# The last gate of a turning cycle behind the next cycle's first sum, with operand, weight and attention work moved to other cycles and steps

## The chip, the cores and the metric

The kernel runs on one core of a Trainium2 chip. The metric is the device time of one execution in microseconds (us); less is better. Engines are named as in the profile: PE multiplies matrices, DVE is the vector engine, ACT the scalar engine, POOL the third elementwise engine, SP the engine that issues all DMAs here.

## What is computed

Chunk attention on 8 x 576 tokens, then two feed-forward layers on the 4608 tokens that come out of it. The reference, cut:

```python
def _attn_ref(q, k, v):                    # q, k, v: 8 x 8 heads x 576 x 64
    chunk = 64
    scores = scale * np.matmul(q_c, k_c.transpose(0, 1, 2, 4, 3))
    attn = np.exp(scores - scores.max(-1, keepdims=True))
    attn = attn / (np.sum(attn, axis=-1, keepdims=True) + 1e-09)
    return np.matmul(attn, v_c).reshape(B, H, S, D)

def _moe_ref(x, w_in, w_out, alpha):       # 4608 x 512, 512 x 2048, 2048 x 512
    h = x @ w_in
    g = np.maximum(h, 0.0) + alpha * np.minimum(h, 0.0)
    return g @ w_out

def _moe2_ref(x, w_in, w_out):
    h = x @ w_in
    return (h - np.tanh(h)) @ w_out
```

The four weight matrices arrive as float64, and the kernel turns each into float32 with integer operations on its words before it uses it.

## The kernel before

Every product is made of three passes: operand and weight are each split into a high part (rounded to the type that PE multiplies fast) and a low part, and high x high, low x high and high x low are summed. The 4608 tokens are 9 blocks of 512; the 2048 features of a layer are 16 groups of 128.

**Layer one, blocks 0 to 6**, is 112 steps. A step multiplies one feature group up (`up`, 12 matmuls, L547) and multiplies the group of two steps earlier down into four accumulators y0 to y3 (`down`, 12 matmuls, L617), through `next_down`. At steps 49, 65, 81 and 97 (and others of that form) the down work is the last of a block, and `finish` copies the four accumulators to stage tiles `yst` (ACT, L642) and stores them to `ysc` (SP, L643). The stage pool has three tiles, which `neg` and `xst` use too, so the fourth copy waits until the first store has landed. All else is woven in by a table: `at(step, fn, ..., place=)` appends to `events[step]`, and `step_one` fires the places 1 and 2, then `up`, place 0, `down`, place 3, the gate `act_g`, the block's stores, and place 4. The table carries

- the attention of the later token tiles: loads into `raw` (`some_loads`, L340, 32 DMAs of SP for a unit of tiles), transposes (`att_a` on DVE, L385; `att_a_natural` on PE, L358, for the tiles 8, 13, 31 and 22, copied by DVE L359 and ACT L360), scores `sc` (L400), weights `p`, and the product with v into `xp` (L471). `tr`, `sc` and `xp` share one PSUM tile pair, tag "a", so each waits for the readers of the last.
- the *parks*: the second layer's weights converted, combined into the seven operands of a fast 2 x 2 block product, split, and written to device memory for later. `park_load` (SP, L206, tile `rw`), `park_form` (DVE conversions, POOL sums L222, L230), `park_split` (ACT L254, POOL L255, tiles `whi`, `mr`), `park_store` (SP, L266). Sixteen of the kinds "u1"/"u" follow each other every four steps from step 36; the first six of kind "d" (weights of the down product) come after them.

**The pair stage** (`two_blocks`) takes two blocks at a time. Pair s=0 is layer one's blocks 7 and 8, s=1 to 4 are layer two's pairs, each of 8 cycles p=0 to 7; eight half-wide cycles (`small`) for the last block follow. A cycle makes four 128 x 512 results from seven products (p1, p5, p6, p2, p3, p7, p4, of 6 matmuls each, L1196) instead of eight. Its sums: `copy` H0 and p5 (ACT, L1206), `add(H1, X, p5)` after p6 and `add(Y, X, p5)` after p7 (DVE, L1203). H1 is what p3 goes on to accumulate in, and X, which add(Y) reads, is what p4 overwrites. Each result goes through a `Gate`: `square`, `second`, `edge` on ACT, `drain` on DVE (L595, L596, which frees the PSUM bank), `close` on DVE (L606 to L608, two inputs in SBUF). The gates are c11, c12, c22 and c21 in this order. Between the products stand 48 down matmuls (24 for s=0), in the numbers that `gaps` gives; a plain cycle of layer two has 12 of them before p4 and 36 after. For s > 0 the cycles p=0 and p=4 are *turning* cycles (`turns`): the accumulators change from one block of the pair to the other, and 12 down matmuls stand ahead of p1's sum and 12 behind it.

`on(s, p, place, fn)` hangs further work on a cycle (`run` fires it): for the next pair `turn`, `put(product, operand)` (two ACT copies L698 and two subtractions L700 for the two halves) and `tokens(o, a, b)` (two subtractions, L710); loads of them (`load_y`); and the last ten "d" parks, one to a cycle. `c21.close()` is the last thing a cycle gives DVE ahead of its `end` hooks, and the next cycle's add(H1) stands behind both.

## Time and profile before

| | us |
|---|---|
| median of three runs | 1693.98 (1693.06 to 1698.06) |
| the profiled execution | 1695.32 |
| its span in the trace | 1693.5 |
| PE busy | 1619.7 (96%) |
| DVE busy | 1232.0 (73%) |
| ACT busy | 986.9 (58%) |
| POOL busy | 458.8 (27%) |

The profiled execution stands 1.34 us above the median. A PE of 96% leaves 74 us in which it was idle; the busy time itself holds matmuls that ran at a lower clock for a while after a gap. The chain of waits, the sum of PE's waits by cause and the start of each cycle's first product tell where these are.

### The profile page before, as it was taken

The page shows a single profiled execution, that of the slowest core. Times are in us where ns is not written, and L with a number is a line of the kernel's source. Part 1 is how long each engine was busy: PE and PEld are TensorE (multiplying, and loading weights), DVE is VectorE, ACT ScalarE, POOL GpSimd, SP SyncE. Part 2 cuts the span into 40 slices and gives each one's busy share as a digit, 9 for nine tenths or more (in the row PEclk, how much of TensorE's full clock was granted, in tenths as well). Part 3 has the DMA queues.
Part 4 walks back from the last instruction along what each step waited for, and adds up shares of the span by engine and source line. Part 5 has one row for each costly group of instructions (what it writes and reads, how often), then busy time and mean ns, then how long its engine had stood idle before and what let it go on. Part 6 is the DMA issues. An engine that isn't in the chain of part 4 may idle for free.

```text
span 1693.5 us, 26409 instructions
## 1 busy us (share of the span) xinstructions
PE 1619.7 (96%) x9309; PEld 1329.5 (79%) x9309; DVE 1232.0 (73%) x1860; ACT 986.9 (58%) x1769; POOL 458.8 (27%) x422
## 2 busy tenths in 40 slices
PE   7899999999999999999899899999999999999999
PEld 6688888878877887888677787787878777878887
DVE  7878857768777787743667788768886877688763
ACT  5756545455554555665566667575766676566553
POOL 1000002444334444322322223122222232222333
PEclk9999999999999999999999999999999999999999
DMA  9451426565565657477678735463555454544650
GB/s 261 153 189 39 107 69 139 131 171 140 141 149 141 153 147 233 146 258 229 217 235 297 250 108 174 139 199 103 181 162 178 127 159 150 164 136 156 216 160 25
DMA packets 339299, 276.49 MB, mean 163 GB/s; under 512 B 180432, under 2 KB 244960, under 8 KB 339168
## 3 DMA queue, kind: packets, MB, share of 16 engines
q1 hardware_dynamic: 339168, 274.82, 54.5%
q8 instruction: 73, 1.20, 0.3%
q14 instruction: 58, 0.48, 0.1%
HBM read 192.95 MB, written 81.79 MB: 162 GB/s over the span
## 4 chain that ended last, share of the span: by engine, by line
PE 69%; DVE 13%; ACT 5%; issue 5%; DMA 4%; SPq 3%; POOL 2%; DVEq 0%; ACTq 0%; POOLq 0%
PE y L1103 23%; PE hps L547 12%; PE y L617 12%; PE hpb L1196 10%; PE hps L1196 10%; SPq L340 2%; DVE arena L607 1%; DVE arena L606 1%; DMA ysc<-yst 1%; DVE g L560 1%; DVE arena L608 1%; DMA rw<-in_moe_w_in_dram 1%; DMA wu<-wu 1%; POOL glo L578 1%; DVE arena L595 1%
## 5 line engine op out<-in xcount | busy, mean ns | idle before, releaser
L578 POOL TENSOR_TENSOR glo<-arena,ghi 128x512 fp32r<-128x512 f32 x145 | 201.3, 1402 | 531.3 <-ACT ghi L575 354.3
L547 PE MATMUL hps<-x,w 128*128 128x512 f32 (+1 forms) x1356 | 328.4, 392 | 5.9 <-ACT kt L374 5.3
L547 PEld LDWEIGHTS hps<-x,w 128*128 128x128 f32 x1356 | 255.4, 190 | 59.6 <-ACT kt L374 5.8
L1103 PE MATMUL y<-w,ghi 128*128 128x512 f32 x1152 | 296.7, 390 | 0.0
L1196 PE MATMUL hpb<-w,wu 128*128 128x512 f32 (+1 forms) x912 | 218.3, 383 | 35.7 <-DVE hpb L1203 32.7
L1103 PEld LDWEIGHTS y<-w,ghi 128*128 128x128 f32 x1152 | 215.4, 188 | 43.7
L617 PE MATMUL y<-ghi,w 128*128 128x512 f32 x880 | 233.0, 398 | 6.3 <-ACT yst L642 6.3
L1196 PEld LDWEIGHTS hpb<-w,wu 128*128 128x128 f32 x912 | 165.9, 192 | 73.6 <-DVE hpb L1203 37.2
L1196 PE MATMUL hps<-w,wu 128*128 128x512 f32 (+1 forms) x912 | 215.7, 382 | 3.6 <-ACT hpb L1206 2.1
L1196 PEld LDWEIGHTS hps<-w,wu 128*128 128x128 f32 x912 | 168.0, 194 | 39.9 <-ACT hpb L1206 4.8
L617 PEld LDWEIGHTS y<-ghi,w 128*128 128x128 f32 x880 | 162.8, 189 | 42.3 <-ACT yst L642 7.6
L1103 PE MATMUL y<-w,glo 128*128 128x512 f32 x576 | 163.2, 390 | 1.0 <-POOL glo L578 1.0
L560 DVE SCALAR_TENSOR_TENSOR g<-neg,nalpha_sb,g 128x512 f32<-128x512 f32 x112 | 94.2, 841 | 54.9 <-ACT g L559 54.8
L617 PE MATMUL y<-glo,w 128*128 128x512 f32 x440 | 126.7, 391 | 0.1
L1103 PEld LDWEIGHTS y<-w,glo 128*128 128x128 f32 x576 | 107.8, 188 | 24.0 <-POOL glo L578 1.8
L578 DVE TENSOR_TENSOR glo<-g,ghi 128x512 fp32r<-128x512 f32 x111 | 95.9, 864 | 34.9 <-ACT ghi L575 33.8
L222 POOL TENSOR_TENSOR whi<-w 128x256 f32<-128x256 f32 x32 | 26.3, 845 | 333.3 <-DMA ysc<-yhalf 234.0
L575 ACT ACTIVATE ghi<-g 128x512 fp32r<-128x512 f32 x112 | 70.5, 630 | 78.2 <-DVE g L560 77.9
L558 ACT ACTIVATE neg<-hps 128x512 f32<-128x512 f32 x112 | 66.3, 592 | 76.9 <-PE hps L547 76.7
L608 DVE COPY_PREDICATED arena<-ktc,th 128x512 f32<-128x512 uint32 x118 | 97.9, 830 | 10.2 <-ACT ktc L602 0.6
L599 ACT ACTIVATE w<-sq,bias_sb 128x512 f32<-128x512 f32 x144 | 104.0, 722 | 0.0
L602 ACT ACTIVATE ktc<-sq,edge_sb 128x512 f32<-128x512 f32 x144 | 103.8, 721 | 0.0
(173 smaller groups left out, 2497.0 us busy)
## 6 DMA issues: line engine op xcount, KB each, us to landing
wu<-wu SPq DMA_DIRECT2D x336, 256.0 KB, 3.2
g<-arena SPq DMA_DIRECT2D x67, 256.0 KB, 3.6
arena<-g SPq DMA_DIRECT2D x65, 256.0 KB, 3.8
raww<-in_moe_w_in_dram SPq DMA_DIRECT2D x16, 512.0 KB, 5.4
v<-in_v_dram SPq DMA_DIRECT2D x32, 256.0 KB, 3.8
raww<-in_moe_w_out_dram SPq DMA_DIRECT2D x16, 512.0 KB, 5.3
rw<-in_moe_w_in_dram SPq DMA_DIRECT2D x16, 512.0 KB, 5.0
wu<-whi SPq DMA_DIRECT2D x32, 256.0 KB, 2.6
```

The lines of the kernel that those rows point to most:

```text
L340: nc.sync.dma_start(out=o, in_=i)
L547: nc.tensor.matmul(out=hp[:, cols], lhsT=w[:, a, m], rhs=x[b][:, kk, cols], start=(kk == 0 and i == 0), stop=(kk == KD - 1 and i == 2),)
L558: nc.scalar.activation(out=neg, in_=hp, func=AF.Relu, scale=-1.0)
L560: nc.vector.scalar_tensor_tensor(out=g, in0=neg, scalar=nalpha_sb[:, f:f + 1], in1=g, op0=ALU.mult, op1=ALU.add)
L575: nc.scalar.activation(out=hi, in_=g, func=AF.Copy)
L578: lo_engine.tensor_tensor(out=lo, in0=g, in1=hi.bitcast(F32), op=ALU.subtract)
L599: nc.scalar.activation(out=self.w, in_=self.sq, func=AF.Square, bias=bias_sb)
L602: nc.scalar.activation(out=self.mask, in_=self.sq, func=AF.Relu, bias=edge_sb)
L608: nc.vector.copy_predicated(g, self.mask.bitcast(U32), self.th)
L617: nc.tensor.matmul(out=acc[t], lhsT=lhsT, rhs=rhs, start=(f == ends[0] and i == 0), stop=(f == ends[1] and i == 2))
L1103: nc.tensor.matmul(out=self.acc[t], lhsT=lhsT, rhs=rhs, start=(self.f == self.ends[0] and i == 0), stop=(self.f == self.ends[1] and i == 2),)
L1196: nc.tensor.matmul(out=o, lhsT=w[:, a, c], rhs=x[c][:, b, :h], start=start and i == 0 and c == 0, stop=i == 2 and c == 1, skip_group_check ...
```

## The change

1. **att_a_natural** of tiles 13, 31 and 22 is fired two steps before the tile's scores instead of one (13: step 29 instead of 30; 31: 56 instead of 57; 22: 65 instead of 66), and the loads of the unit behind it may begin a step sooner. `some_loads` leaves out the steps 49, 65, 81 and 97.
2. **Parks of kind u**: the load moves from place 4 of a step to place 2 of the next, form and split of "u1" from place 2 to place 4 of the step before, and the store of "u" from place 4 to place 1 of its step. At a block's end that puts it, and the load, ahead of the block's `ysc` stores on SP.
3. **Border of s=0**: `turn`, put p1 and two `tokens` move from the last cycle to the end of the one before; the other operands are spread over p6, p7, p4 and the end of the last cycle, all on DVE, with two extra tile pairs e1 and e2.
4. **Borders of s >= 1**: `turn` and put p1 move from the end of p=4 to the end of p=5, a `tokens` from the end of p=5 to that of p=6, and the puts of p7 and p4 from the places p1 and p2 of the next pair's first cycle to its place p6.
5. **The ten last "d" parks** run three to two cycles, all within s=0 (before: one to a cycle, the last three in s=1, p=1 to 3).
6. **A turning cycle's** `c21.close()` and its `enlist` are put on `ends` and done in the next cycle, right behind add(H1).

```diff
@@ -755,14 +755,18 @@
     for unit in units:
         t = unit[0]
         if t % 9 == 4:
-            at(base[t] - 1, att_a_natural, t)
+            early = 1 if t < 3 * NPT else 2
+            at(base[t] - early, att_a_natural, t)
             at(free, load_natural_late, t)
-            free, apart = base[t], 1
+            free, apart = base[t] - early + 1, 1
         else:
             turn, apart = base[t] - (1 if t == 11 else apart), 2
             at(free, begin_unit, t, len(unit))
-            for r in range(free, turn):
-                at(r, some_loads, -(-32 // max(1, turn - 1 - free)))
+            loading = [r for r in range(free, turn) if r < 2 * KF or r % KF != 1]
+            loading = loading[:max(1, turn - 1 - free)]
+            for r in loading:
+                at(r, some_loads, -(-32 // len(loading)))
+            at(turn - 1, some_loads, 64)
             for i, tt in enumerate(unit):
                 at(turn + i, att_a, tt)
             free = turn + len(unit)
@@ -798,13 +802,13 @@
     at(2 * KF + 4, park_desk)
     for i in range(KF):
         n, c, step = i // 2, i % 2, 2 * KF + 4 + 4 * i
-        at(step, park_load, "u", n, c, place=4)
-        at(step + 2, park_form, "u1", n, c, place=2)
-        at(step + 2, park_split, "u1", n, c, place=2)
+        at(step + 1, park_load, "u", n, c)
+        at(step + 1, park_form, "u1", n, c)
+        at(step + 1, park_split, "u1", n, c)
         at(step + 3, park_store, "u1", n, c, place=4)
         at(step + 3, park_form, "u", n, c)
         at(step + 4, park_split, "u", n, c)
-        at(step + 5, park_store, "u", n, c, place=2 if i == KF - 1 else 4)
+        at(step + 5, park_store, "u", n, c, place=1)
     DP = 6
     for f in range(DP):
         step = 6 * KF + 5 + 2 * f
@@ -1241,44 +1245,45 @@
                 for name in names:
                     xs[m, name] = xs[m - 1, name]
 
+        V, G = nc.vector, nc.gpsimd
+
         def parks_done():
             spare.append(tuple(wide.tile([P, 2, 512], F32R, tag="w", name="xo") for _ in range(2)))
             new_slots(wide.tile([P, 2, 512], F32, tag="r", name="slots", bufs=1))
-
-        V, G = nc.vector, nc.gpsimd
+            raw["e1"] = [att.tile([P, NB], F32, tag=tag, name="e1") for tag in ("p", "pt")]
+            raw["e2"] = [vpool.tile([P, NB], F32, tag="v", name="e2") for _ in range(2)]
 
         def border(s):
             m = s + 1
             if s == 0:
                 on(s, 5, "p1", load_y, m, "b11", "b12")
                 on(s, 6, "p1", load_y, m, "b22", "b21")
-                on(s, 7, "start", turn, m)
-                for place, fn, args in (
-                    ("p1", put, ("p1", "b11", V)), ("p1", tokens, ("b11", "b12", "b11", V)),
-                    ("p5", put, ("p5", "b11", V)), ("p5", tokens, ("b11", "b22", "b11", V)),
-                    ("p6", put, ("p6", "b11", V)),
-                    ("p2", put, ("p2", "b21", V)), ("p2", tokens, ("b21", "b21", "b11", V)),
-                    ("p3", tokens, ("b12", "b22", "b12", V)), ("p3", put, ("p3", "b22", G)),
-                    ("p7", put, ("p7", "b12", G)),
+                on(s, 6, "end", parks_done)
+                on(s, 6, "end", turn, m)
+                for p, place, fn, args in (
+                    (6, "end", put, ("p1", "b11", V)), (6, "end", tokens, ("b11", "b12", "b11", V)),
+                    (6, "end", tokens, ("b12", "b22", "b12", V)),
+                    (7, "p6", put, ("p5", "b11", V)), (7, "p6", tokens, ("e1", "b22", "b11", V)),
+                    (7, "p7", put, ("p6", "e1", V)), (7, "p7", tokens, ("e2", "b21", "e1", V)),
+                    (7, "p4", put, ("p2", "b21", V)), (7, "end", put, ("p3", "b22", V)),
+                    (7, "end", put, ("p7", "b12", V)), (7, "end", put, ("p4", "e2", V)),
                 ):
-                    on(s, 7, place, fn, m, *args)
-                on(s, 7, "p3", drop, "b11")
-                on(s, 7, "p7", drop, "b22")
-                on(s, 7, "p7", drop, "b12")
-                on(s, 7, "end", put, m, "p4", "b21", V)
-                on(s, 7, "end", drop, "b21")
+                    on(s, p, place, fn, m, *args)
+                on(s, 7, "p7", drop, "b11")
+                on(s, 7, "end", drop, "b21", "b22", "b12")
+                on(s, 7, "end", lambda: [raw.pop(name) for name in ("e1", "e2")])
                 return
             on(s, 4, "p1", load_y, m, "b11", "b12")
             on(s, 5, "start", load_y, m, "b22", "b21")
-            on(s, 4, "end", turn, m)
-            on(s, 4, "end", put, m, "p1", "b11", V)
+            on(s, 5, "end", turn, m)
+            on(s, 5, "end", put, m, "p1", "b11", V)
             on(s, 5, "end", tokens, m, "b11", "b12", "b11", V)
-            on(s, 5, "end", tokens, m, "b12", "b22", "b12", V)
+            on(s, 6, "end", tokens, m, "b12", "b22", "b12", V)
             on(s, 6, "end", tokens, m, "e1", "b22", "b11", V)
             on(s, 6, "end", tokens, m, "e2", "b21", "e1", V)
             for p, place, product_, name in (
                 (7, "p1", "p5", "b11"), (7, "end", "p6", "e1"), (7, "end", "p2", "b21"), (7, "end", "p3", "b22"),
-                (8, "p1", "p7", "b12"), (8, "p2", "p4", "e2"),
+                (8, "p6", "p7", "b12"), (8, "p6", "p4", "e2"),
             ):
                 on(s + p // 8, p % 8, place, put, m, product_, name, V)
                 on(s + p // 8, p % 8, place, drop, name)
@@ -1289,14 +1294,17 @@
             border(s)
         on(0, 0, "start", park_load, "d", DP, 0)
         on(0, 0, "p5", park_store, "d", DP - 1, 0)
+        slips = (
+            (0, "p2", "p7", 0, "p4", 0, "p3"), (0, "end", "p6", 1, "p2", 1, "start"), (1, "p7", "end", 0, "start", 1, "p4"),
+        )
         for i, f in enumerate(range(DP, KF)):
-            s, p = (0, i) if i < 7 else (1, i - 6)
-            on(s, p, "p2", park_form, "d", f, 0)
+            p, form, split, later, store, latest, load = slips[i % 3]
+            p += 2 * (i // 3)
+            on(0, p, form, park_form, "d", f, 0)
+            on(0, p + later, split, park_split, "d", f, 0)
+            on(0, p + latest, store, park_store, "d", f, 0)
             if f + 1 < KF:
-                on(s, p, "p3", park_load, "d", f + 1, 0)
-            on(s, p, "p4", park_split, "d", f, 0)
-            on(s, p, "end", park_store, "d", f, 0)
-        on(1, 4, "start", parks_done)
+                on(0, p + (load == "start"), load, park_load, "d", f + 1, 0)
 
         def cycle(s, p):
             X, Y, H0, H1 = banks2 if p % 2 == 0 else banks2[2:] + banks2[:2]
@@ -1315,6 +1323,8 @@
             downs(gaps[0])
             product(s, "p6", X, NB)
             add(H1, X, p5)
+            while ends:
+                ends.pop(0)()
             run(s, p, "p6")
             downs(gaps[1])
             if turns:
@@ -1359,8 +1369,15 @@
             c21.edge()
             c22.close()
             enlist(s, 1, 2 * p + 1, c22.g)
-            c21.close()
-            enlist(s, 0, 2 * p + 1, c21.g)
+
+            def finish():
+                c21.close()
+                enlist(s, 0, 2 * p + 1, c21.g)
+
+            if turns:
+                ends.append(finish)
+            else:
+                finish()
             run(s, p, "end")
             if p == NPAIR - 1:
                 line.extend(right[s])
```

The rows below are the order in which an engine meets its instructions; tile numbers differ between the two builds. L1207 of the changed kernel is L1203 of the kernel before.

DVE from the end of s=3, p=4 (a turning cycle) into p=5, before: close of c22 left out, close of c21 (first three rows), put p1, add(H1), c11's drain, add(Y).

```order
L606 SCALAR_TENSOR_TENSOR arena_6844<-w_12356,arena_6844 128x512
L607 SCALAR_TENSOR_TENSOR arena_6844<-sq2_8650,arena_6844 128x512
L608 COPY_PREDICATED arena_6844<-ktc_101,th_12357 128x512
L700 TENSOR_TENSOR w_1425<-arena_7628,w_1425 128x512
L700 TENSOR_TENSOR w_1514<-arena_6844,w_1514 128x512
L1203 TENSOR_TENSOR hpb_7625<-hps_7626,ptb_102 128x512
L595 SCALAR_TENSOR_TENSOR slots_9390<-sq2_8650,hpb_7624 128x512
L596 TENSOR_TENSOR th_12434<-hpb_7624,th_12434 128x512
L1203 TENSOR_TENSOR hps_7627<-hps_7626,ptb_102 128x512
```

The same after: close of c22 (first three rows), add(H1), close of c21, drain, add(Y).

```order
L606 SCALAR_TENSOR_TENSOR arena_6846<-w_12342,arena_6846 128x512
L607 SCALAR_TENSOR_TENSOR arena_6846<-sq2_8692,arena_6846 128x512
L608 COPY_PREDICATED arena_6846<-ktc_101,th_12343 128x512
L1207 TENSOR_TENSOR hpb_7625<-hps_7626,ptb_102 128x512
L606 SCALAR_TENSOR_TENSOR arena_7628<-w_12360,arena_7628 128x512
L607 SCALAR_TENSOR_TENSOR arena_7628<-sq2_8692,arena_7628 128x512
L608 COPY_PREDICATED arena_7628<-ktc_101,th_12361 128x512
L595 SCALAR_TENSOR_TENSOR slots_8538<-sq2_8692,hpb_7624 128x512
L596 TENSOR_TENSOR th_12434<-hpb_7624,th_12434 128x512
L1207 TENSOR_TENSOR hps_7627<-hps_7626,ptb_102 128x512
```

The put is gone from here, to the end of p=5, and c21's close stands between add(H1) and add(Y).

SP at the block end of step 97, before: park load, a v load, four loads of the next pair, the block's four stores, then the park's two stores.

```order
L206 DMA rw_2783<-in_moe2_w_in_dram 128x2x256
L301 DMA v_6842<-in_v_dram 128x8x64
L693 DMA arena_6844<-xsc7_3515 128x512 x4
L643 DMA ysc5_6915<-yst_6916 128x512
L643 DMA ysc5_6915<-yst_6919 128x512
L643 DMA ysc5_6915<-yst_6922 128x512
L643 DMA ysc5_6915<-yst_6925 128x512
L266 DMA wu1_7_6835<-whi_2784 896x1x128
L266 DMA wu1_7_6835<-mr_2785 896x1x128
```

The same place of SP after the change:

```order
L266 DMA wu1_7_6835<-whi_2784 896x1x128
L266 DMA wu1_7_6835<-mr_2785 896x1x128
L301 DMA v_6843<-in_v_dram 128x8x64
L206 DMA rw_2783<-in_moe2_w_in_dram 128x2x256
L693 DMA arena_6846<-xsc7_3515 128x512 x4
L643 DMA ysc5_6917<-yst_6918 128x512
L643 DMA ysc5_6917<-yst_6921 128x512
L643 DMA ysc5_6917<-yst_6924 128x512
L643 DMA ysc5_6917<-yst_6927 128x512
```

The park's two stores are now the first of the row, and the block's four the last.

PE around step 29 before the change: the end of a down, the up of the step, the product xp of tile 11, the next down; the transposes of tile 13 come a step later.

```order
L617 MATMUL y2_2173<-glo_2193,w_1425 128x512
L617 MATMUL y3_2174<-glo_2193,w_1425 128x512
L547 MATMUL hps_2321<-x_648,w_1514 128x512 x12
L471 MATMUL xp_2334<-ptb_102,v_2155 64x64 x16
L617 MATMUL y0_2171<-ghi_2249,w_1514 128x512
L617 MATMUL y1_2172<-ghi_2249,w_1514 128x512
```

PE at the same place after the change:

```order
L617 MATMUL y2_2173<-glo_2193,w_1425 128x512
L617 MATMUL y3_2174<-glo_2193,w_1425 128x512
L547 MATMUL hps_2321<-x_648,w_1514 128x512 x12
L358 MATMUL tr_2335<-ident_96,rawn_2148 128x128 x8
L471 MATMUL xp_2346<-ptb_102,v_2155 64x64 x16
L617 MATMUL y0_2171<-ghi_2249,w_1514 128x512
L617 MATMUL y1_2172<-ghi_2249,w_1514 128x512
```

The transposes `tr` of tile 13 stand between the up and xp, and all three share the PSUM pair "a" with the scores.

## Rows read from the trace of the kernel before

**Rows 1.** PE's waits: line, releaser, total us, count, longest us.

```profile
PE hpb L1196 <- DVE hpb L1203: 32.7, 10, 5.1
PE y L617 <- ACT yst L642: 6.3, 3, 3.6
```

**Rows 2.** PE timeline (start, us, instruction): first products of the pair stage's parts.

```profile
719.47 4.56 PE L1196 MATMUL hpb<-w,wu 128*128 128x512 f32 x18
...
847.80 1.52 PE L1196 MATMUL hpb<-w,wu 128*128 128x512 f32 x6
...
1555.73 1.48 PE L1196 MATMUL hpb<-w,wu 128*128 128x256 f32 x11
```

**Rows 3.** PE timeline: s=3, p=5 with its p3 late; starts of p=6, p=7.

```profile
1313.15 1.52 PE L1196 MATMUL hps<-w,wu 128*128 128x512 f32 x6
...
1318.24 1.54 PE L1196 MATMUL hpb<-w,wu 128*128 128x512 f32 x6
1323.22 2.38 PE L1196 MATMUL hpb<-w,wu 128*128 128x512 f32 x6 [3.44 <-DVE hpb L1203]
...
1339.94 1.52 PE L1196 MATMUL hpb<-w,wu 128*128 128x512 f32 x6
...
1360.34 1.52 PE L1196 MATMUL hps<-w,wu 128*128 128x512 f32 x6
```

**Rows 4.** DVE timeline around the same stall, and at the end of p=6.

```profile
1316.63 0.76 DVE L608 COPY_PREDICATED arena<-ktc,th 128x512 f32<-128x512 uint32 x1
...
1317.99 1.68 DVE L607 SCALAR_TENSOR_TENSOR arena<-sq,arena 128x512 f32<-128x512 f32 x1
1319.77 1.62 DVE L608 COPY_PREDICATED arena<-ktc,th 128x512 f32<-128x512 uint32 x1
1321.29 1.27 DVE L700 TENSOR_TENSOR w<-arena,w 128x512 fp32r<-128x512 f32 x2
1322.48 0.68 DVE L1203 TENSOR_TENSOR hpb<-hps,ptb 128x512 f32<-128x512 f32 x1
...
1361.18 2.48 DVE L710 TENSOR_TENSOR arena<-arena 128x512 f32<-128x512 f32 x4
1363.58 1.28 DVE L700 TENSOR_TENSOR w<-arena,w 128x512 fp32r<-128x512 f32 x2
```

**Rows 5.** POOL timeline in the same stretch.

```profile
1319.08 1.71 POOL L578 TENSOR_TENSOR glo<-arena,ghi 128x512 fp32r<-128x512 f32 x1
```

**Rows 6.** The page's groups: POOL's splits (count, busy us, mean ns, idle before).

```profile
L578 POOL TENSOR_TENSOR glo<-arena,ghi 128x512 fp32r<-128x512 f32 x145 | 201.3, 1402 | 531.3 <-ACT ghi L575 354.3
```

**Rows 7.** PE timeline in layer one: steps 49, 56, 70 and 97.

```profile
350.81 0.99 PE L617 MATMUL y<-ghi,w 128*128 128x512 f32 x2 [3.58 <-ACT yst L642]
...
385.80 1.98 PE L617 MATMUL y<-ghi,w 128*128 128x512 f32 x8
...
473.09 0.69 PE L400 MATMUL sc<-ktc,qt 64*64 64x64 f32 x32 [3.91 <-DVE ktc L385]
...
646.20 0.73 PE L617 MATMUL y<-ghi,w 128*128 128x512 f32 x2 [0.60 <-ACT yst L642]
```

**Rows 8.** DVE timeline at step 56.

```profile
387.71 0.69 DVE L521 TENSOR_TENSOR x<-sc,x 128x512 fp32r<-128x512 f32 x1 [1.19 <-ACT x L517]
```

**Rows 9.** ACT timeline: copy behind tile 8's transposes; a park's split near step 70.

```profile
228.36 0.60 ACT L360 ACTIVATE ktc<-tr 128x512 f32<-128x512 f32 x1 [4.88 <-DVE qt L359]
...
468.08 0.95 ACT L254 ACTIVATE whi<-mr 128x896 fp32r<-128x896 f32 x1 [6.42 <-DMA wu<-whi]
```

**Rows 10.** The chain of waits: first store of a block, steps 49 and 97.

```profile
344.03 6.03 DMA ysc<-yst
...
640.53 4.92 DMA ysc<-yst
```

**Rows 11.** DMA issues on the page: count, size, median us to landing.

```profile
ysc<-yst SPq DMA_DIRECT2D x16, 256.0 KB, 3.2
```

**Rows 12.** POOL timeline: a park's low parts before step 97.

```profile
638.23 2.14 POOL L255 TENSOR_TENSOR mr<-mr,whi 128x896 fp32r<-128x896 f32 x1 [1.06 <-ACT whi L254]
```

## The prediction

> **What bounds the kernel now.** PE is busy for 96% of the span, so only the time that PE loses can be won. I read PE's waits first: one line stands far above the others, the products of the pair stage that wait for DVE's add at L1203, ten times, 32.7 us in all, 5.1 at the longest [rows 1]. Next come the down products that wait for ACT's copies at block ends, 6.3 us. Idle time is not all: matmuls behind a gap run slower, so I measure whole stretches against what their matmuls take when dense. A plain cycle of layer two runs from 1339.94 to 1360.34, 20.40 us [rows 3], for 42 + 48 = 90 matmuls, 0.2267 us each. Layer two's 32 cycles should take 32 x 20.40 = 652.8, and take 1555.73 - 847.80 = 707.93 [rows 2]: **55.1 us lost**. The 8 cycles of s=0 have 42 + 24 = 66 matmuls, 14.96 us each, 119.7 in all, and take 847.80 - 719.47 = 128.33: **8.6 us lost**. Together 63.7 us, in which the waits of L1203 are about half.
>
> One such cycle shows how it comes about: s=3, p=5, right behind a turning cycle, takes 1313.15 to 1339.94 = 26.79, which is 6.4 too long [rows 3]. Its p2 begins at 1318.24, so p6 ended there and add(H1) could have begun. But DVE does c21's close first, whose L607 and L608 take 1.68 and 1.62, then the put for the next pair, 1.27; add(H1) starts only at 1322.48 [rows 4], and p3 waits 3.44 us for it. Behind the gap p3's six matmuls take 2.38 instead of 1.52, as the next six do. There are eight such cycles, p=1 and p=5 of four pairs; 8 x 6.4 = 51 is about what layer two loses. So the stalls there come from one place in DVE's order, not from too much work.
>
> **Parts 4 and 6, layer two.** In the new order add(H1) stands directly behind c22's close. That close ended at 1316.63 + 0.76 = 1317.39 [rows 4]; p6 ends at 1313.15 + 18 x 0.2267 = 1317.2 at the earliest. The add takes 0.68, so its result is there at 1318.1. Between p6 and p3 stands p2 alone, 1.36 us: p3 is due at 1318.6 or later. The stall of 3.4 should vanish, and with it the slow matmuls. What is late next is **add(Y)**: it comes behind c21's close and c11's drain now. From add(H1)'s end, c21's three operations take 2.1 to 2.3 undisturbed (the L608 that ran alone took 0.76); with two of them beside POOL, 1.68 + 1.62 + 0.7, they take 4.0. The drain is two more of the add's kind, 1.3, the add itself 0.7: add(Y) ends 4.1 to 6.0 after add(H1). p4, which overwrites X, is due after p3, p7 and 12 down matmuls, 24 x 0.2267 = 5.4, plus the 0.5 between the add's end and p3. So the stall at p4 lies between 0 and 0.1 when all is as in this trace. I take 0.5 us for each of the eight cycles for jitter and small waits of the copies, 4 us (bounds 0 and 12).
>
> The hooks that leave p=4's end go to others. At p=5's end now stand put p1 and one tokens, four DVE operations ahead of p=6's add(H1), 1.28 + 1.24 = 2.5 us: four tokens operations ran there before without a wait (p=6 took 20.40, [rows 3]), so 0.4 each for three or four borders, 1.5 us. At p=6's end three tokens instead of two, eight operations with the put of p5 in p=7's place p1: before, 2.48 + 1.28 [rows 4] ended at 1364.86, where add(H1) began, and p3 was due at 1360.34 + 24 x 0.2267 = 1365.8. A further 1.24 and the add's 0.7 bring 1366.8: about 1 us late, 1.5 with the slow matmuls behind it. Three times, 4.5 us (0 to 9). The next pair's p=0 loses two puts ahead of its add(H1) and gets them behind p6, where they stand ahead of c11's drain, with their four ACT copies ahead of c11's square. Behind p6 of a turning cycle stand 12 down matmuls and p2, 18 x 0.2267 = 4.1 us, before c11 can start, so the 2.6 us of DVE and about as much of ACT are hidden; were that cover gone, 2 us a border. The waits of p=0 fall.
>
> **Parts 3 and 5, layer one's pair.** In s=0 the last cycle holds the whole loss of 8.6. With the put of p1 and two tokens at p=6's end, and the rest spread on DVE instead of POOL, I leave 0.5 us and gain 8. The ten conversions fall in s=0, three to two cycles; the last three left s=1, where they cost their share of the 55. In s=0 DVE has no drains and a close of one operation per gate, so 1.5 conversions a cycle find room: they come with a load of 512 KB and two stores each on SP and two copies on ACT, of which I charge nothing while PE's products cover them, and 3 us where they don't.
>
> Sum for the pair stage: 63.7 - 4 - 1.5 - 4.5 - 0.5 - about 1 of other remains = **52 us gained** (35 to 60).
>
> **Parts 1 and 2, layer one.** Here the change moves things ahead of what PE waits for.
> - Step 29: the transposes of tile 13 come between the up and xp, in the same PSUM pair. xp must wait for both copies; for tile 8 the ACT copy started at 228.36, after the DVE copy, and ended 228.96 [rows 9], some 1.6 us after its transposes. Before, xp followed the up directly. Cost 1.5 (0 to 2).
> - (Leaving out four steps in the loads changes nothing where no loads are left by then.) Step 56: the up ends at 385.80 [rows 7], where the transposes of tile 31 now stand; their PSUM pair is read by DVE L521 until 387.71 + 0.69 = 388.40 [rows 8]. PE waits 2.6 us, 3 with slow matmuls. Step 65: the same pattern, its readers done; 0.
> - Step 49: y waits 3.58 for the copy [rows 7], which waits for the first store: issued at 344.03, landed 6.03 later [rows 10], where the median is 3.2 [rows 11], since the park's load (512 KB) and v (256 KB) are ahead. The change puts two stores of 448 KB ahead as well. At (6.03 - 3.2) / 768 KB = 3.7 ns per KB, 896 KB cost 3.3; I take 3 (0 to 4).
> - Step 70: `sc` waits 3.91 [rows 7] because ACT stood at a park's split until 468.08, for a store behind 32 loads on SP [rows 9]. The loads still stand ahead and begin after the last ysc store of step 65, which is some 1.5 us later: 1.5 (-4 to 3).
> - Step 97: the wait is 0.60 [rows 7], with the store issued at 640.53 and landed 4.92 later [rows 10]. In the new order SP issues first the park's `mr`, which POOL finishes at 638.23 + 2.14 = 640.37 [rows 12], then v, the load and four arena loads: eight issues of about 0.5 before the first ysc store, which so lands about 650: 4.5 (0 to 6). Step 81 has its park stores in the same place: 1 (0 to 3).
>
> Sum: 1.5 + 3 + 3 + 1.5 + 4.5 + 1 = 14.5, say **14 us lost** (0 to 20). Net -52 + 14 = -38: 1695.3 - 38 = 1657 for an execution like the profiled one, which is 1.3 above the median; **1656 us**.
>
> **The rivals.**
> *The wait moves to p4* (1676). The closing trio runs longer than in rows 4, because all three of its operations, whose inputs both lie in SBUF, fall beside POOL's split of 1.4 us mean [rows 6]. L608 took 0.76 alone and 1.62 beside POOL [rows 4, 5]. If each of the three waits out a whole POOL operation, 2.1 + 3 x 1.4 = 6.3, then 1.3 and 0.7 give 8.3 against 5.9 due, so p4 is 2.4 late: 8 x 2.5 = 20 us of the gain are gone, 1656 + 20 = 1676. For it: POOL's splits of the turning cycle's groups run at this place. Against: only two of three fell beside POOL in rows 4, and POOL idles 531 us ahead of these splits. The Trainium skill ("SBUF — State Buffer", section "Who interferes with whom") says that a DVE instruction with two SBUF inputs contends with a GpSimd instruction that reads SBUF, and that whoever issues first holds the shared ports for its whole instruction; the trace's 1.68 and 1.62 agree in kind. By that rule the price is this rival's.
>
> *Layer one loses nothing* (1642). The three stalls, 3.6, 3.9 and 0.6 [rows 7], stay or shrink since the earlier park stores free `whi` and `mr` sooner and the loads begin earlier: 1656 - 14 = 1642, less with a stall gone. For it: the tile `whi` was what ACT waited for at step 70. Against: the orders of SP in all four block ends put bytes ahead of the store that PE waits for.
>
> *DVE becomes the bound of each cycle* (1706, slower). A cycle of layer two has four gates of five DVE operations and two adds, 22 instructions of 0.64 (half of the put's 1.28) to 0.76 [rows 4], 14 to 16.7 us, say 15.3, under 20.40. Each of the 12 closing operations grows by 1 us beside POOL. From 6.5 us on, seven of twelve, a cycle takes 21.8 in all of 32, the 32 x 1.4 = 45 lost eat the gain, and with 14 in layer one the kernel is slower; at 22.3 it is 1695 - 64 + 32 x 1.9 + 14 = 1706. Against: POOL has 145 such splits [rows 6] in 40 cycles, 3.6 of 1.4 us each, which can't cover seven.
>
> *The change doesn't do what it says*: the deferral helps p3, but the sums and puts shift the same work into other cycles at full price, and only 20 of the 52 us come: 1656 + 32 = 1688.
>
> **How the numbers follow.** Forecast 0.55 (1644 to 1670); p4 late 0.17 (1670 to 1684); layer one free 0.17 (1632 to 1644); no effect 0.07; DVE bound 0.04. The range holds the first whole, most of the second and third: 1637 to 1682. A measurement of this kernel tells about 0.3%, 5 us, from no change. Faster takes the first three and part of the fourth: 0.90; within 0.3% 0.05; slower 0.05.
>
> **What would show it.** In the new trace the waits for DVE's add at p3 fall from 32.7 us to under 8, the cycles p=1 and p=5 take 20.4 to 21.5, and p=7 up to 22. The last cycle of s=0 takes about 15.5. PE's waits for `yst` grow from 6.3 to about 14, at steps 49 and 97. It is wrong if the cycles p=1 and p=5 still take over 23 (where p4 waits, rival one), or if the block ends' waits don't grow (rival two).

## The result, and the profile after

The changed kernel takes **1652.86 us** (four runs, 1651.27 to 1654.08) against 1694.13 before: 0.9752 of it, 95% interval 0.9734 to 0.977. The forecast was 1656. The profiled execution took 1653.5, its span 1651.5.

The page's line of busy time, and PE's waits (engine, line, releaser: us in all, times, longest us), to be read beside [rows 1]; L1207 is the add that was L1203 before, L1200 the products that were L1196:

```profile
PE 1608.0 (97%) x9309; PEld 1326.2 (80%) x9309; DVE 1218.6 (74%) x1864; ACT 989.2 (60%) x1769; POOL 452.0 (27%) x418
...
PE y L617 <- ACT yst L642: 6.2, 2, 4.2
...
PE hpb L1200 <- DVE hpb L1207: 4.8, 4, 2.4
PE sc L400 <- DVE ktc L385: 4.8, 1, 4.8
PE tr L358 <- issue: 2.5, 1, 2.5
```

The wait for DVE's add fell from 32.7 us to 4.8. PE's busy time fell by 11.7 us for the same 9309 matmuls, since fewer of them run at the lower clock behind a gap. The first products of the stage's parts (PE timeline: start, us, instruction), beside [rows 2]:

```profile
728.83 3.41 PE L1200 MATMUL hpb<-w,wu 128*128 128x512 f32 x13
...
836.76 2.88 PE L1200 MATMUL hps<-w,wu 128*128 128x512 f32 x12
...
856.87 1.52 PE L1200 MATMUL hpb<-xo,wu 128*128 128x512 f32 x6
...
1514.13 1.12 PE L1200 MATMUL hpb<-w,wu 128*128 128x256 f32 x8
```

| stretch, us | before | after | measured | forecast |
|---|---|---|---|---|
| all up to the pair stage | 719.47 | 728.83 | +9.4 | +14 |
| s=0 | 128.33 | 128.04 | -0.3 | about -8 |
| s=1 to 4 | 707.93 | 657.26 | -50.7 | about -44 |
| pair stage together | 836.26 | 785.30 | -51.0 | -52 |

Of the 50.7 us of layer two, 45.0 come from the eight cycles p=1 and p=5, 5.5 from p=0, where p4 had waited for ACT behind the puts, and 3.5 from p=2 and p=3 of s=1, which have no conversions now; the cycles p=7 take 3.3 back. The first seven of the eight half-wide cycles take 13.28 us each in both.

**Where the gain is.** The stretch of [rows 3] and [rows 4] in the changed kernel, s=3, p=5: first DVE, then PE.

```profile
1291.67 0.76 DVE L608 COPY_PREDICATED arena<-ktc,th 128x512 f32<-128x512 uint32 x1
1292.68 0.70 DVE L1207 TENSOR_TENSOR hpb<-hps,ptb 128x512 f32<-128x512 f32 x1 [0.24 <-PE hps L1200]
1293.29 0.86 DVE L606 SCALAR_TENSOR_TENSOR arena<-w,arena 128x512 f32<-128x512 f32 x1
1294.18 1.67 DVE L607 SCALAR_TENSOR_TENSOR arena<-sq,arena 128x512 f32<-128x512 f32 x1
1295.89 0.76 DVE L608 COPY_PREDICATED arena<-ktc,th 128x512 f32<-128x512 uint32 x1
...
1297.73 0.69 DVE L1207 TENSOR_TENSOR hps<-hps,ptb 128x512 f32<-128x512 f32 x1
```

```profile
1288.20 2.88 PE L1200 MATMUL hps<-w,wu 128*128 128x512 f32 x12
...
1292.41 2.88 PE L1200 MATMUL hpb<-w,wu 128*128 128x512 f32 x12
1295.13 1.52 PE L1200 MATMUL hps<-w,wu 128*128 128x512 f32 x6
...
1299.21 1.52 PE L1200 MATMUL hps<-w,wu 128*128 128x512 f32 x6
```

The add starts at 1292.68, and now DVE waits for PE (0.24), not PE for DVE. p2 and p3 run as one group of twelve from 1292.41. The closing trio follows the add, one of its operations at 1.67, and add(Y) ends at 1297.73 + 0.69 = 1298.42, before p4 starts at 1299.21: **0.8 us to spare**. All eight cycles p=1 and p=5 take 20.53 to 20.59 us, with one operation of the trio at 1.67 and 0.79 to 0.84 us to spare in each; before, they took 24.3 to 27.7, 209.3 in all. In the p=5 cycles of before a smaller wait went as well, which the prediction doesn't name: p6, which overwrites X, waited up to 0.71 us for ACT's copy of H0, which stood behind put p1's two ACT copies.

```profile
1316.74 1.66 PE L1196 MATMUL hps<-w,wu 128*128 128x512 f32 x6 [0.71 <-ACT hpb L1206]
```

**Where layer one pays.** PE's stalls of steps 29, 49, 56, 70 and 97, beside [rows 7]:

```profile
225.65 0.69 PE L471 MATMUL xp<-ptb,v 64*64 64x64 f32 x32 [1.41 <-ACT ktc L360]
...
355.87 1.22 PE L617 MATMUL y<-ghi,w 128*128 128x512 f32 x2 [4.21 <-ACT yst L642]
...
394.61 1.06 PE L358 MATMUL tr<-ident,rawn 128*128 128x128 f32 x8 [2.54 <-issue]
...
484.41 1.13 PE L400 MATMUL sc<-ktc,qt 64*64 64x64 f32 x32 [4.78 <-DVE ktc L385]
...
655.59 0.73 PE L617 MATMUL y<-ghi,w 128*128 128x512 f32 x2 [2.03 <-ACT yst L642]
```

Two are new (1.41 and 2.54), three have grown (3.58 to 4.21, 3.91 to 4.78, 0.60 to 2.03), and a wait of 2.1 at step 81 is gone. For the stall of 2.54 the profile names no releaser ("issue"); DVE's last reading of the PSUM pair ends at 394.50, just ahead of the transposes:

```profile
393.81 0.69 DVE L521 TENSOR_TENSOR x<-sc,x 128x512 fp32r<-128x512 f32 x1 [1.18 <-ACT x L517]
```

Of the 9.4 us that layer one is longer, 2.9 belong to no part of the change: they arise at 75 us, where both kernels do the same and PE waits equally long, before and after in turn:

```profile
75.36 3.01 PE L547 MATMUL hps<-x,w 128*128 128x512 f32 x12 [2.62 <-ACT kt L374]
```

```profile
75.49 5.49 PE L547 MATMUL hps<-x,w 128*128 128x512 f32 x12 [2.65 <-ACT kt L374]
```

The same twelve matmuls took 3.01 us at a granted clock of 1.00 and 5.49 at 0.50. Step 29 is the first at which the change moves work of PE; in the traces of the kernels below it starts between 216.3 and 220.6 us (217.5 before, 220.5 in the changed kernel). Each kernel was traced once, so it isn't shown how far this varies between executions of one kernel. Two traces can differ by some 4 us ahead of step 29 for no reason in the edit, so what an edit did is read here stall by stall.

### The profile page after: what moved, and what is told of

Same layout as the page of the kernel before. It is cut to its first block, busy times and chain, and to the rows that moved or that the text cites. A ratio compares the mean times of both kernels' runs of the same rounds, so it can differ in the third digit from the quotient of the medians.

```text
span 1651.5 us, 26382 instructions
## 1 busy us (share of the span) xinstructions
PE 1608.0 (97%) x9309; PEld 1326.2 (80%) x9309; DVE 1218.6 (74%) x1864; ACT 989.2 (60%) x1769; POOL 452.0 (27%) x418
## 5 line engine op out<-in xcount | busy, mean ns | idle before, releaser
L578 POOL TENSOR_TENSOR glo<-arena,ghi 128x512 fp32r<-128x512 f32 x147 | 206.4, 1419 | 505.7 <-ACT ghi L575 355.2
L1200 PE MATMUL hpb<-w,wu 128*128 128x512 f32 (+1 forms) x888 | 205.3, 374 | 5.5 <-DVE hpb L1207 4.8
L1200 PE MATMUL hps<-w,wu 128*128 128x512 f32 (+1 forms) x888 | 205.1, 375 | 1.5 <-ACT hpb L1210 1.4
L1200 PEld LDWEIGHTS hpb<-w,wu 128*128 128x128 f32 x888 | 158.7, 189 | 37.9 <-DVE hpb L1207 6.5
L1200 PEld LDWEIGHTS hps<-w,wu 128*128 128x128 f32 x888 | 158.8, 189 | 34.7 <-ACT hpb L1210 4.8
L560 DVE SCALAR_TENSOR_TENSOR g<-neg,nalpha_sb,g 128x512 f32<-128x512 f32 x112 | 90.8, 811 | 78.6 <-ACT g L559 78.4
L607 DVE SCALAR_TENSOR_TENSOR arena<-sq,arena 128x512 f32<-128x512 f32 x119 | 103.0, 865 | 4.1
L608 DVE COPY_PREDICATED arena<-ktc,th 128x512 f32<-128x512 uint32 x119 | 93.2, 783 | 10.5 <-ACT th L591 0.5
```

Of the source, the lines that this page charges most:

```text
L560: nc.vector.scalar_tensor_tensor(out=g, in0=neg, scalar=nalpha_sb[:, f:f + 1], in1=g, op0=ALU.mult, op1=ALU.add)
L578: lo_engine.tensor_tensor(out=lo, in0=g, in1=hi.bitcast(F32), op=ALU.subtract)
L607: nc.vector.scalar_tensor_tensor(out=g, in0=self.sq, scalar=TS[0], in1=g, op0=ALU.add, op1=ALU.mult)
L608: nc.vector.copy_predicated(g, self.mask.bitcast(U32), self.th)
L1200: nc.tensor.matmul(out=o, lhsT=w[:, a, c], rhs=x[c][:, b, :h], start=start and i == 0 and c == 0, stop=i == 2 and c == 1, skip_group_check ...
```

## The experiments

**What the deferral does, and what the put does.** Two kernels take part 6 and the rest of the change apart. The first undoes part 6 in the changed kernel:

```diff
-            if turns:
-                ends.append(finish)
-            else:
-                finish()
+            finish()
```

> The changed kernel with part 6 undone: c21's close again stands ahead of the next cycle's add(H1) in every cycle, while the puts and tokens stay where the change has them. My theory, that the closing trio ahead of the add is the larger share of the loss: after c22's close it takes 2.2 to 4.0 us, the add another 0.7, so p3 is 1.6 to 3.4 us late with 0.9 to 1.7 of slow matmuls behind it, in the eight cycles p=1 and p=5 of s=1 to 4, 20 to 36 us in all: 1673 to 1689. Rival, that the put ahead of the add was what made it late: the cycles stay at 20.5 and the time below 1656.

Measured: 1693.95 us (ratio 1.0007, interval 0.9988 to 1.0026): not a part of the gain is left. DVE and PE in s=3, p=5 of this kernel:

```profile
1319.28 1.66 DVE L607 SCALAR_TENSOR_TENSOR arena<-sq,arena 128x512 f32<-128x512 f32 x1
1321.05 1.61 DVE L608 COPY_PREDICATED arena<-ktc,th 128x512 f32<-128x512 uint32 x1
1322.56 0.69 DVE L1207 TENSOR_TENSOR hpb<-hps,ptb 128x512 f32<-128x512 f32 x1
```

```profile
1323.30 2.93 PE L1200 MATMUL hpb<-w,wu 128*128 128x512 f32 x6 [3.11 <-DVE hpb L1207]
```

The put is gone from here, and p3 still waits 3.11 us, since the trio with two operations beside POOL stands ahead of the add. The add is some 1.2 us earlier, counted from the cycle's p1 (8.13 us behind it, 9.33 before); the eight cycles take 208.0 us against 209.3. The theory was right in kind and short in size: 1673 to 1689 was expected. The pair stage does gain 6.1 here (1556.62 - 726.42 = 830.2), but layer one is 7.0 longer.

The second puts part 6 alone into the kernel before (the new lines in the cycle; nothing else of the change):

```diff
             add(H1, X, p5)
+            while ends:
+                ends.pop(0)()
...
-            c21.close()
-            enlist(s, 0, 2 * p + 1, c21.g)
+            def finish():
+                c21.close()
+                enlist(s, 0, 2 * p + 1, c21.g)
+
+            if turns:
+                ends.append(finish)
+            else:
+                finish()
```

> The kernel before with part 6 alone. Theory: the four p=1 cycles fall from 24.3 to 27.2 us to 20.5, the four p=5 cycles, where the put stays ahead of the add, to about 21.5; 40 of the 46 us above 20.40 go, all else stays: about 1655. Rival, that the wait only moves to p4: the cycles stay above 22.5 and the time above 1672.

Measured: 1657.26 us (0.9788, 0.9769 to 0.9806). One edit of a few lines brings 36 of the 41 us. The waits for the add fall from ten of 32.7 us to six of 7.9, of which 5.1 is the border of s=0. In s=3, p=5, where the put is still ahead of the add:

```profile
1293.10 2.39 DVE L700 TENSOR_TENSOR w<-arena,w 128x512 fp32r<-128x512 f32 x2
1295.41 0.69 DVE L1203 TENSOR_TENSOR hpb<-hps,ptb 128x512 f32<-128x512 f32 x1
```

```profile
1296.15 1.65 PE L1196 MATMUL hpb<-w,wu 128*128 128x512 f32 x6 [0.55 <-DVE hpb L1203]
```

Here the put met POOL, and took 2.39 instead of 1.27; p3 waits 0.55, p6 still waits its 0.71 for ACT's copy, and the cycle takes 22.27. The four p=1 cycles, without a put, take 20.7 (23.1 in s=1, which still has a conversion there, so that p4 waits 1.42 for add(Y): the rival's wait, in one cycle). So the pair stage is 836.3 before, 830.2 with all but the deferral, 800.5 with the deferral alone and 785.3 with both: 6.1 + 35.8 = 41.9 apart, 51.0 together. The parts help each other. With the deferral in place the other parts bring 6.4 us in the p=5 cycles, from which the put goes, and 3.1 in the p=1 cycles, most of it where the conversion goes; without the deferral they bring 1.4 and nothing there, since a put that is moved away from behind a trio uncovers only the trio.

**How near p4 is.** Three more copies under mask behind each deferred close:

```diff
                 c21.close()
+                if turns:
+                    for _ in range(3):
+                        nc.vector.copy_predicated(c21.g, c21.mask.bitcast(U32), c21.th)
```

> The changed kernel with three more copies under mask (L608 again, the same result) behind each deferred close, 0.65 us apart. In the trace add(Y) ends 0.8 us before p4 is due. Theory: 1.95 - 0.8 = 1.15 us of wait at p4, 0.3 of slow matmuls, eight times: 11 to 12 us more, about 1664. Rival, that p4 has other cover: 1653; or that slow matmuls behind the gap double the price: 1675.

Measured in one run: 1672.62. PE in this kernel, p4 of s=3, p=5 and p3 of p=6:

```profile
1313.31 1.65 PE L1200 MATMUL hps<-w,wu 128*128 128x512 f32 x6 [1.46 <-DVE hps L1207]
...
1329.65 1.65 PE L1200 MATMUL hps<-w,wu 128*128 128x512 f32 x6 [1.07 <-DVE hps L1207]
```

p4 waits 1.46, so the wait does move to p4 as soon as the 0.8 us are used up; the cycles take 22.3, 1.8 more, 14 in all. What no theory had: p=6 waits too, in three of four pairs, 21.8 instead of 20.4. DVE carries the delay through p=5, meets the put and tokens at its end, and is late for the next add. That makes the other 4 us. The time lies near the dearer rival (1675), though not by its mechanism.

**Layer one.** Parts 1 and 2 undone together, in the lines of the first two hunks of the diff:

> The changed kernel with parts 1 and 2 undone, so that layer one's steps are those of before. Theory, that these parts lose: the traces put 6.4 us more of stalls at steps 29 to 97 into the changed kernel, so 1646 to 1647. Rival, that they are needed for the rest or neutral: 1652 to 1654 or more.

Measured: 1639.73 us (0.9689, 0.9663 to 0.9714), 13 us better than the changed kernel. The stalls at 29, 56, 81 and 97 are absent, the one at step 49 is 3.4 and that of step 70 4.2 us. From step 29 to step 97 it takes 8.3 us less than the changed one: 8 of the 13. Another 1.4 lie ahead of step 29, in no part, and 3.3 in the last cycle of s=0, which took 16.8 instead of 20.1 with the same code in it. Why it is shorter is seen at the border of s=0, below.

Part 1 undone alone:

```diff
-            early = 1 if t < 3 * NPT else 2
+            early = 1
```

> The changed kernel with the transposes of tiles 13, 31 and 22 back at one step before their scores. Theory, that they wait for the PSUM pair at the earlier place: the losses of 1.5 us at step 29 and 4.4 at step 56 go, 1647. Rival, that the wait belongs to the step and not to the transposes, or comes back at the loads behind: 1652 to 1654.

Measured: 1648.5 us (0.9733, 0.9713 to 0.9754). The two stalls are gone, 5.9 us with their slow matmuls, as expected. But the block ends wait more (7.9 us in three waits instead of 6.2 in two) and step 70 too (5.3 instead of 4.8), so steps 29 to 97 together are only 2.2 us shorter in the trace. A further 1.3 lie in the last cycle of s=0, which the edit doesn't touch.

The parks' stores and loads behind the block's stores:

```diff
-        at(step + 1, park_load, "u", n, c)
+        at(step + 1, park_load, "u", n, c, place=4 if (step + 1) % KF == 1 else 2)
...
-        at(step + 5, park_store, "u", n, c, place=1)
+        at(step + 5, park_store, "u", n, c, place=4 if (step + 5) % KF == 1 and i < KF - 1 else 1)
```

> The changed kernel in which the park's store and load at the steps 49, 65, 81 and 97 stand behind the block's stores on SP. Theory, that bytes and issues ahead of the first store make PE wait: step 97 loses 2.3 less, step 49 (7.1 now) 3 to 5 less, step 70 about 1.5 less: 1645 to 1650. Rival, that the landing of the first store doesn't depend on what is ahead: 1652 to 1654.

Measured: 1642.42 us (0.9701, 0.9683 to 0.972), 10 us better than the changed kernel. PE's wait for `yst` at step 49 falls from 4.21 to 0.21 and the one at step 97 is gone: what stands ahead of the first store on SP is the price. At step 49 it is paid in two ways: counted from step 29, SP issues the first store 2.3 us earlier here, and it lands 3.31 us after its issue instead of 5.05. At step 70 the wait grew from 4.8 to 6.9 instead of falling. The 10 us are not all the edit's own: in the trace steps 29 to 97 are 6.5 us shorter, 4.1 lie ahead of them, and 1.4 in the last cycle of s=0.

**The border of s=0.** POOL, DVE and PE in the last cycle of s=0 of the changed kernel:

```profile
841.21 3.16 POOL L578 TENSOR_TENSOR glo<-arena,ghi 128x512 fp32r<-128x512 f32 x2 [7.25 <-ACT ghi L575]
```

```profile
841.46 1.79 DVE L710 TENSOR_TENSOR slot<-arena,slot 128x512 f32<-128x512 f32 x1
843.17 1.75 DVE L710 TENSOR_TENSOR arena<-arena 128x512 f32<-128x512 f32 x1
844.85 0.69 DVE L1207 TENSOR_TENSOR hpb<-hps,ptb 128x512 f32<-128x512 f32 x1
```

```profile
845.59 2.39 PE L1200 MATMUL hpb<-w,wu 128*128 128x512 f32 x6 [2.42 <-DVE hpb L1207]
```

Two subtractions ahead of the add run beside POOL and take 1.79 and 1.75 where their like takes 0.69. In the experiment they move behind the add:

```diff
-                    (6, "end", tokens, ("b12", "b22", "b12", V)),
...
+                    (7, "p4", tokens, ("b12", "b22", "b12", V)),
```

> The changed kernel with two of the four subtractions that stand ahead of add(H1) in the last cycle of s=0 moved to the place p4 of that cycle. In the trace they take 1.79 and 1.75 beside POOL, and p3 waits 2.4 us. Theory: the wait and its slow matmuls, 4.3 us, go: the cycle falls from 20.1 to 16, the time to 1649. Rival, that the loss goes to the end of the cycle, where the puts for the next pair's p3, p7 and p4 queue up: no gain.

Measured in one run: 1647.51; the cycle takes 15.67 and p3 doesn't wait. In the traces s=0 is 3.6 us shorter than in the changed kernel; the other 2.5 lie in layer one, which the edit doesn't touch. In the kernel with layer one's parts undone one of the two subtractions stood clear of POOL, p3 waited 1.3 us and the cycle took 16.8. DVE and POOL there:

```profile
831.38 0.68 DVE L710 TENSOR_TENSOR slot<-arena,slot 128x512 f32<-128x512 f32 x1
831.98 1.78 DVE L710 TENSOR_TENSOR arena<-arena 128x512 f32<-128x512 f32 x1
```

```profile
831.40 3.50 POOL L578 TENSOR_TENSOR glo<-arena,ghi 128x512 fp32r<-128x512 f32 x2 [6.92 <-ACT ghi L575]
```

The subtraction that started 0.02 us ahead of POOL's split took 0.68; in the changed kernel it started 0.25 us behind the split and took 1.79. The clock matters nearly as much as POOL. In the kernels with part 1 undone, with the parks behind and with the subtractions at p=7 moved (below), p3 of this cycle waits the same 2.4 us, and the cycle takes 18.3 to 18.8 instead of 20.1. Behind the wait the granted clock was 0.65 to 0.67 for 5 us in the changed kernel (from 845.5), and 1.00 in the last of these (from 846.6).

**The six subtractions at p=6's end:**

```diff
-            on(s, 6, "end", tokens, m, "e2", "b21", "e1", V)
+            on(s, 7, "p6", tokens, m, "e2", "b21", "e1", V)
```

> The changed kernel with the last two of six subtractions at the end of p=6 moved behind add(H1) of p=7, for s=1 to 4. Theory: the three p=7 cycles of 21.5 us fall to 20.4 to 20.5, 3.2 us, 1650. Rival, that they are then late for the next pair's puts: p=0 grows by as much.

Measured in one run: 1649.76; the three p=7 cycles take 20.40 instead of 21.5, and p=0 stays at 20.40.

**All together.** The four edits of natural_undone, parks_behind, border0 and tokens7 in one kernel:

> The changed kernel with four of the single edits together: transposes back at one step ahead, park stores and loads behind the block's stores at the block ends, two subtractions of s=0's border at p4, two of the later borders behind add(H1) of p=7. Theory, that they add up: the waits at steps 29, 49, 56 and 97 are gone (some 13 us), the border of s=0 gives 3 to 4, p=7 gives 3.2, step 70 stays at 6 to 8: 1632 to 1635. Rival, that waits only change places between steps: 1640 or more.

Measured: 1631.06 us (0.963, 0.9609 to 0.9651), 21.8 below the changed kernel, where the single gains (4.4, 10.4, 5.4 and 3.1) make 23.3. They add up about, though not each for its own reason: some of the single gains lay ahead of step 29 or in the last cycle of s=0. In the trace of this kernel 13.1 us come in steps 29 to 97, 3.5 in s=0, 3.0 in layer two and 3.2 ahead of step 29. The waits for `yst`, for the transposes and for DVE's add in the pair stage are gone from the trace. What is left of layer one is step 70. ACT there:

```profile
464.29 0.95 ACT L254 ACTIVATE whi<-mr 128x896 fp32r<-128x896 f32 x1 [8.12 <-DMA wu<-whi]
```

It waits 8.12 us for a park's store behind 32 loads on SP, as in [rows 9]. The last experiment takes that store ahead of them:

```diff
-        at(step + 3, park_store, "u1", n, c, place=4)
+        at(step + 3, park_store, "u1", n, c, place=1)
```

> The same, with the store of each u1 park at place 1 instead of place 4 of its step, ahead of the second half of the 32 loads on SP. Theory, that the wait at step 70 comes from that store standing behind the loads: ACT's split no longer waits 6 to 8 us, PE's wait at step 70 falls from 5 to 7 to under 1: 1626 to 1629. Rival, that the loads themselves land too late there: as the kernel without this edit.

Measured: 1629.66 us (0.9627, 0.961 to 0.9643), no clear difference to the last, as the rival said. ACT, DVE and PE of this kernel:

```profile
456.19 0.96 ACT L254 ACTIVATE whi<-mr 128x896 fp32r<-128x896 f32 x1
```

```profile
467.61 0.71 DVE L385 STREAM_TRANSPOSE ktc<-raw 128x512 f32<-128x512 f32 x1 [6.03 <-DMA raw<-in_k_dram]
```

```profile
468.47 1.13 PE L400 MATMUL sc<-ktc,qt 64*64 64x64 f32 x32 [5.17 <-DVE ktc L385]
```

ACT waits no more, and PE still waits 5.17: now the last k load lands too late. The edit itself has made it late. It puts the store ahead of all 32 loads, not of their second half, and SP holds it until POOL has its data; the loads begin at 450.12 instead of 441.42, and SP needs 15.8 us to issue 32 of them. SP without the edit, then with it, and POOL with it:

```profile
441.42 10.14 SPq L340 DMA_DIRECT2D raw<-in_q_dram  x16
```

```profile
448.29 1.74 SPq L266 DMA_DIRECT2D wu<-whi  x2
450.12 7.90 SPq L340 DMA_DIRECT2D raw<-in_q_dram  x16
```

```profile
447.31 0.95 POOL L252 CAST whi<-whi 128x512 fp32r<-128x512 f32 x1
```

Without the edit DVE doesn't wait for a load (its transposes start at 467.86, behind ACT's split), so my reading of [rows 9], that the split's wait is what holds PE there, stands for that kernel, and this experiment doesn't refute it. A store in the middle of the loads was not tried.

## Why the prediction was right

**The main step held.** With the add behind c22's close only, p3 no longer waits, and the slow matmuls behind it go. What was late next was add(Y), as said, with 0.8 us left where I had put it between 0.1 late and 1.8 early. The trio met POOL once in this trace, not twice. I charged 0.5 us for each of the eight cycles; they lost 0.13 to 0.19, from a small wait of p6 for a copy. The rival that the wait moves to p4 didn't come. It was near: the 0.8 us to spare are less than one more meeting with POOL costs (1.67 against 0.76 or less), and the slack experiment shows that p4 is what waits next. The rule of the Trainium skill ("SBUF — State Buffer", section "Who interferes with whom"), that a DVE instruction with two SBUF inputs contends with a GpSimd (here POOL) instruction that reads SBUF and that one of the two holds the ports for its whole instruction, agrees in kind with the 1.67 here and the 1.79 and 1.75 at the border.

**The hooks.** p=7 cost 1.1 us in each of three pairs against 1.5 forecast: the add at the end of eight operations made p3 wait 0.80.

```profile
1335.53 1.66 PE L1200 MATMUL hpb<-w,wu 128*128 128x512 f32 x6 [0.80 <-DVE hpb L1207]
```

p=6 cost nothing, where 1.5 in all was charged, and p=0 fell to 20.40 in all four pairs, from 20.55 to 22.45, as said.

**The border of s=0 was mis-sized.** I left 0.5 us for it; its cycle takes 20.1, 5.1 too long. The step that failed is that I counted the work moved to the end of p=6 as free. It is six DVE operations ahead of an add, the same pattern as at p=5 of layer two, which I had just described, and two of them met POOL; slow matmuls behind the wait made up the rest. The first seven cycles of s=0 grew by 107.9 - 105.3 = 2.6, within the 0 to 3 that I allowed for the denser conversions. In layer two all four charges were too high: 11 us in all, where 4.5 are left. The two errors, 7.7 us in s=0 and 6.7 the other way in layer two, cancel. That the pair stage came out within 1 us of the forecast is luck in the sizes, not in the mechanism.

**Layer one, step by step.** Step 29: 1.41 waited against 1.5. Step 56: 2.54 against 2.6, with slow matmuls 4.4 instead of 3. Step 70: 0.9 more against 1.5. Step 49: 0.6 more wait and 1.7 more loss, against 3. Step 97: 1.4 more against 4.5. Step 81: 2.1 less, 2.4 with slow matmuls, against 1 more. With their slow matmuls these make 7.4 us, not 14; three steps between 569 and 599 us of the kernel before are 0.9 shorter together, without a wait in either trace, and with the 2.9 us at 75 us, which no part explains, it is 9.4. I had named a sign of being wrong here, that the block ends' waits don't grow, and by it this part failed: the waits for `yst` are 6.2 us in all where they were 6.3 and I expected 14. They grew at steps 49 and 97, by 2.1 together, and the one at step 81 went. Three terms failed:

- Step 49. I let the bytes ahead make the first store land 3 us later. It landed 5.05 us after its issue, sooner than before (6.03); what grew was the time of its issue, 350.07, some 1.6 us later when the 4.4 us by which the kernel runs behind are taken off.

- Step 97. I took the end of POOL's work on the park, 640.37, from the trace of before, and let SP wait for it. But part 2 moves the park's earlier work too, and POOL was done sooner:

```profile
641.66 2.13 POOL L255 TENSOR_TENSOR mr<-mr,whi 128x896 fp32r<-128x896 f32 x1 [1.06 <-ACT whi L254]
```

It ends at 643.79, where the kernel runs some 8 us behind the one before, so some 4.5 us earlier in the program. SP issued the first store at 648.55, no later than before in the same terms. What grew was its landing, 6.3 us instead of 4.92, behind the park's bytes and the loads.

- Step 81. The third copy of the block ended its wait for a different reason. ACT before, and after:

```profile
549.44 1.09 ACT L642 ACTIVATE yst<-y 128x512 f32<-128x512 f32 x2 [3.82 <-DMA ysc<-yst]
```

```profile
557.26 1.20 ACT L642 ACTIVATE yst<-y 128x512 f32<-128x512 f32 x2 [2.68 <-DVE g L560]
```

Before, this copy got the stage tile of the first copy and had to wait for its store; in the changed kernel it got that of `neg`, and the fourth copy the stored one. At the other block ends both kernels have the second form. Which tile a request gets is decided when the program is built, and my reading is that the moved instructions around it turned the choice. Other traces bear on it: with layer one's parts undone, and with the parks' stores and loads alone behind the block's stores, the third copy again waits for a store, but only 1.76 and 1.64 us instead of 3.82, and PE doesn't wait. So the choice does go with the parks' place on SP, and the choice alone doesn't cost the 2.1 us: the first store landed after 4.17 us before and after 2.12 with the parts undone. Why it landed so late before stays open.

**The rivals.** Layer one free of losses (1642) was wrong for the kernel as it stands; the runs with its parts undone, 1639.7, show about what the kernel is worth without them. That the sums and puts only shift their work (1688) didn't come: of the new places only p=7 and the border of s=0 cost anything. DVE as a bound of each cycle didn't come: busy time fell by 13 us. But in the cycles with hooks DVE has little left, as the delay handed on to p=6 in the slack experiment shows.

## What to carry to other kernels

Look for the instruction that a waiting engine needs, and ask of each instruction ahead of it in the same queue who needs that and when: here three instructions that nobody waited for yet stood ahead of one that PE waited for eight times, and putting them behind it brought 36 us. When work is moved out of one such place, check that it isn't put into another of the same kind (the ends of p=6 here), and count what a block's end has ahead of it in the DMA queue in bytes. Moves that bring little while the larger cover still stands can be worth much more once it is gone: try them on both sides of it.

## What the runs showed of the hardware

- A DVE subtraction with both inputs in SBUF took 0.69 us alone and 1.75 to 1.79 beside POOL's split; a put of two took 1.27 or 2.39. One that started 0.02 us ahead of the split took 0.68, the same one 0.25 us behind it 1.79. With this and the clock, the same code in s=0's last cycle took 16.8 to 20.5 us in different kernels, where 14.96 is dense.
- A gap of 2.6 us ahead of the same twelve matmuls at 75 us was followed by a granted clock of 1.00 in one trace and 0.50 in another (3.01 or 5.49 us). Behind the stalls in layer two the cost of slow matmuls varied in the same way: the eight cycles took 24.3 to 27.7 us for waits of 3.3 to 3.5.
